# A long-convolution and FFN kernel: K tables by 128 x 80 matmuls, transforms in 64-row tiles, one chain for 640 channels, and a fixed order of steps

## Chip, cores and metric

The kernel runs on one core of one Trainium2 chip. The metric is the device time of one execution in microseconds (us). Executions of one kernel differ by 1 to 2%. A few runs are marked slow (over 1.5% above the fastest of their kernel); comparisons here are of fast runs with fast runs.

Engine names as in the profile: PE is the TensorE matmul, PEld its weight load (which overlaps PE), DVE is VectorE, ACT is ScalarE, POOL is GpSimd, SP is the engine that issues the DMAs (SPq: its queue of issues). "L678" is line 678 of the kernel that the line is taken from, so the same work has different line numbers in different kernels.

## The reference, cut to what matters

```python
# u: [1, 2048, 640];  L = 2048, D = 640 channels, N = 128 states, F = 1728
g = sigmoid((x * gate_w).sum(-1))                       # x = u
K = einsum("dn,dnl,dn->dl", C, exp(dt * A * l), dt * B).real   # a kernel of 2048 taps for each channel
y = irfft(rfft(u padded) * rfft(K padded))[:L] + u * Dskip     # long convolution
b = (gelu(x @ w_gate) * (x @ w_up)) @ w_down            # GeGLU FFN
out = g * y + (1 - g) * b
```

The kernel makes K from two tables by a contraction over the 128 states, with one small product for each group of channels. It then does the convolution by a transform in two stages (A and B), multiplies the spectra of u and K ("mix"), and transforms back (the end of the mix, then "finish"). FFN work fills PE in between.

## The kernel before: the parts that matter

The program is a list of steps. Each has a cost, what it reads and writes, and a rank. A list scheduler inside the kernel's build replays the steps with these costs and writes them out in the order that results; the ranks are the dictionary `P`.

```python
def contract(h):                              # h: half of the channels, W = 320
    ...
                for i in range(16):
                    for q in range(2):
                        for cg in range(4):
                            c = 16 * (b0 + b) + i
                            nc.tensor.matmul(ps[32 * cg:32 * cg + NE, k + b, 32 * i:32 * i + 32],
                                             lhsT=cs2[:, q, c, cg:4 * NE:4],      # 128 x 20 stationary
                                             rhs=cs1[:, q, c, cg:128:4],          # 32 moving columns
                                             start=(q == 0), stop=(q == 1))
    ...                                       # 640 matmuls for a half, 1280 in all
    for e0, n, r0, rs in ((0, 8, 1, 8), (8, 4, 257, 4), ...):        # 5 groups
        for cg in range(4):                   # 20 writes, in runs of 80 channels = 160 bytes
            ... nc.sync.dma_start(out=dst, in_=src)     # dS (in HBM) <- K table

def gathers(h, R): ...                        # 15 reads of dS: spread K over the partitions (Kl)
def stageA(h, R): ...                         # first stage of K's transform, write dKA[h]

def stageB(src, key, dst, name, c, R):        # second stage: 128 x 128 weights
    ...
                for b in range(2):
                    nc.tensor.matmul(ps[:, k + b, 0:W], lhsT=TB[:, 0, :], rhs=bi[s][:, 2 * a + b, :], start=True, stop=True)

u_spec(0, P["U0"])                            # spectrum of u, half 0
stageA(1, P["A1"])
chain(0, P["C0"]); finish(0, P["F0"])         # mix and back transform, half 0
u_spec(1, P["U1"])
chain(1, P["C1"]); finish(1, P["F1"])         # then half 1
plan.run()                                    # the list scheduler fixes the order
plan.emit()
```

Of the kernel before, what the change touches and what calls it, by code (L numbers as in the profile page):

```python
# [12 lines left out]
I32 = mybir.dt.int32  # L13
# [8 lines left out]
X2 = [1, 2, 3, 4, 5, 6, 7, 8, 258, 260, 262, 264, 516, 520, 772, 776, 1032, 1288, 1544, 1800]  # L22
NE = len(X2)


class Plan:
# [50 lines left out]
    def run(self):  # L77
        S = self.steps
        left = [len(s["deps"]) for s in S]
        succ = [[] for _ in S]  # L80
        for s in S:
            for d in s["deps"]:
                succ[d].append(s["i"])
        free, done, aset, line = {}, {}, None, 0
        cand = {}
        ready = {}
        pairs = [0.0] * 4
        owner = {}
        last = None
        warm, cols, wend = False, 0, 3413  # L90

        def arrive(i):
            s = S[i]
            for e in s["engs"]:
                t = 0
                for d in s["deps"]:
                    same = S[d]["eng"] == e and not S[d]["x"]
                    t = max(t, done[d] + (0 if same else S[d]["lat"]))
                ready[i, e] = t
                cand.setdefault(e, set()).add(i)  # L100

        for s in S:
            if not s["deps"]:
                arrive(s["i"])
        order = []
        INF = 1e18
        while len(order) < len(S):
            best = None
            for e, c in cand.items():
                if not c:  # L110
                    continue
                pmin = min(pairs) if e == "PE" else 0
                m = min((max(ready[i, e], pmin) if S[i]["psum"] else ready[i, e]) for i in c)
                t = max(m, free.get(e, 0))
                if best is None or t < best[0]:
                    best = (t, e, pmin)
            t, e, pmin = best
            assert t < INF, "deadlock"
            pick = None
            for i in cand[e]:  # L120
                s = S[i]
                rd = max(ready[i, e], pmin) if s["psum"] else ready[i, e]
                if rd > t:
                    continue
                sc = s["rank"] - s["age"] * (t - ready[i, e]) / 1000
                if s["aset"] not in (None, aset) and e == "ACT":
                    sc += self.switch
                if pick is None or (sc, i) < pick:
                    pick = (sc, i)
            s = S[pick[1]]  # L130
            i = s["i"]
            for e2 in s["engs"]:
                cand[e2].discard(i)
            s["eng"] = e
            s["t"] = t
            ns = s["engs"][e]
            if e == "ACT" and s["aset"] not in (None, aset):
                ns += 1280
                aset = s["aset"]
            if e == "DVE" and last in s["deps"]:  # L140
                ns += 60
            if e == "DVE":
                last = i
            if s["psum"]:
                p = min(range(4), key=lambda q: (pairs[q], q))
                s["k"] = 2 * p
                pairs[p] = INF
                owner[i] = p
            if e == "PE":
                while t >= wend:  # L150
                    warm = cols >= 3072
                    cols = 0
                    wend += 3413
                    if t >= wend + 3413:
                        warm, wend = False, t - t % 3413 + 3413
                rest, ns = ns, 0
                while rest > 0:
                    rate = 1 if warm else 0.5
                    room = wend - t - ns
                    step = min(rest, room * rate)  # L160
                    cols += s["cr"] * step
                    rest -= step
                    ns += step / rate
                    if rest > 0:
                        warm, cols, wend = cols >= 3072, 0, wend + 3413
            free[e] = done[i] = t + ns
            if s["x"]:
                line = max(line, t + ns) + s["x"]
                done[i] = line
            if s["frees"] is not None:  # L170
                f = S[s["frees"]]
                if all(d in done for d in f["rel"]):
                    pairs[owner[f["i"]]] = max(done[d] for d in f["rel"]) + 150
            order.append(s)
            for d in succ[i]:
                left[d] -= 1
                if not left[d]:
                    arrive(d)
        self.order = sorted(order, key=lambda s: (s["t"], s["i"]))
        self.done = done  # L180
        return max(done.values())

    def emit(self):
        for s in self.order:
            s["fn"](s)
# [3 lines left out]
def kernel(  # L189
# [26 lines left out]
    out3 = out.rearrange("b (m p) d -> (b m) p d", p=NPH)  # L216
# [5 lines left out]
    ARENA = 212224  # L222
    arena = mp.tile([128, ARENA // 2], BF16, name="arena")
    ps = pp.tile([128, 8, 512], FP32, name="ps")
    P = dict(sw=5.4, gate=1.91, up=2.5, gelu=8.59, age=0.75, mul=-0.94, un=1.65, uw=1.85, K0=2.33, K1=5.9,
             W=6.08, RT=6.44, ua=0.33, ue=6.48, down=2.99, z=2.89, T2=2.96, A0=6.55, U0=-3.8, A1=2.03, C0=-4.3,
             F0=0.78, U1=1.3, C1=1.89, F1=0.8)
    plan = Plan(P["sw"])
    add = plan.add
# [30 lines left out]
    def mm(n):  # L260
        return n / 2.4 + 4
# [10 lines left out]
    def dma(kb, fn, r=(), w=(), rank=5.0, **k):  # L272
        return add({"SP": 450}, lambda s: fn(), r, w, rank=rank, lat=1900, x=max(100, kb * 3.2), **k)
# [31 lines left out]
    O_TB = O_W + 5120  # L305
    O_WA = O_TB + 768
    O_CS1 = O_WA + 8192
    O_CS2 = O_CS1 + 40960
    O_TRIG = O_CS2 + 25600
    O_PH = O_TRIG + 10240  # L310
    O_A = O_PH + 20480
    O_TAIL = O_A + 8960
# [6 lines left out]
    Wg = [at(O_W + 1280 * k, [128, NKT, 128], BF16, f"Wg{k}") for k in range(2)]  # L319
    Wu = [at(O_W + 2560 + 1280 * k, [128, NKT, 128], BF16, f"Wu{k}") for k in range(2)]  # L320
    TB = at(O_TB, [128, 3, 128], BF16, "TB")
# [16 lines left out]
    vrdt = at(O_TAIL, [N, D], BF16, "vrdt")  # L338
    drow = at(O_TAIL + 1280, [128, D], BF16, "drow")[0:1]
    krow = [drow[:, W * h:W * h + W] for h in range(2)]  # L340
    kst = at(O_TAIL + 2560, [128, 32, 80], BF16, "kst")
    un = at(O_TAIL + 7680, [128, D], BF16, "un")
    ua = [at(O_TAIL + 8960 + 2560 * k, [128, 2, D], BF16, f"ua{k}") for k in range(2)]
    O_TT = O_ZA
    tph = at(O_TT, [128, 2, 512], I32, "tph")
    tsn = at(O_TT + 4096, [128, 2, 512], BF16, "tsn")
    iot = at(O_TT + 6144, [128, 640], I32, "iot")
    tpb = at(O_TT + 8704, [128, 3, 128], I32, "tpb")
# [5 lines left out]
    i4 = cp.tile([128, 4], I32, name="i4")  # L354
    mA = cp.tile([128, 4], FP32, name="mA")
    mQ = cp.tile([128, 4], FP32, name="mQ")
# [8 lines left out]
    dU = [dp.tile([32, 128, W], BF16, name=f"dU{h}") for h in range(2)]  # L365
    dS = [dp.tile([NS, W], BF16, name=f"dS{h}") for h in range(2)]
    dKA = [dp.tile([32, 128, W], BF16, name=f"dKA{h}") for h in range(2)]
    dY = [dp.tile([32, 128, W], BF16, name=f"dY{h}") for h in range(2)]


    kI = iot[:, 0:32]
    tI = iot[:, 32:48]
    k2I = iot[:, 48:112]
    pI = iot[:, 112:240]
    rI = iot[:, 240:368]

    def iotas():
        g = nc.gpsimd
        g.iota(row_i[:], pattern=[[0, 1]], base=0, channel_multiplier=1)
        g.iota(i4[:], pattern=[[1, 4]], base=0, channel_multiplier=0)  # L380
        g.iota(kI, pattern=[[32, 32]], base=8, channel_multiplier=0)
        g.iota(tI, pattern=[[1, 16]], base=0, channel_multiplier=16)
        g.iota(k2I, pattern=[[1, 64]], base=0, channel_multiplier=0)
        g.iota(pI, pattern=[[1, 16], [0, 2], [16, 4]], base=0, channel_multiplier=0)
        g.iota(rI, pattern=[[0, 16], [16384, 2], [0, 4]], base=0, channel_multiplier=0)
        g.memset(ones[:], 1.0)

    pool(2500, iotas, w=["iot", "ones", "ci"])
    jI = tpb.rearrange("p a b -> p (a b)")

    FIELDS = ((0, 3), (5, 31), (0, 31), (3, 31), (2, 1), (0, 63), (6, 1))

    def fields():
        v = nc.vector
        v.memset(b_eps[:], 1e-37)
        for c, (sh, mask) in enumerate(FIELDS):
            v.tensor_scalar(out=fi[:, c:c + 1], in0=row_i[:], scalar1=sh, scalar2=mask, op0=ALU.logical_shift_right,
# [33 lines left out]
    for pl in range(4):  # L431
        ve(v2(1024), lambda pl=pl: expandA(pl), r=["tsn", "fld"], w=[("WA", pl)], rank=RT)
# [278 lines left out]
    def kgen(h):  # L711
        for g in range(4):
            exps1(h, 4 * g, 4)
# [262 lines left out]
```

## Time and profile before

| | before |
|---|---|
| time, median of 3 runs (range) | 345.71 us (344.22 to 348.69) |
| span of the profiled run, granted clock | 344.3 us, 0.92 |
| PE / DVE / ACT busy | 273.3 / 238.2 / 220.5 us |
| DMA queue | 60.23 MB, 61.1% of 16 engines' span |
| instructions on PE: matmuls, weight loads | 2785, 2798 |

These lines are from the page of the kernel before. In part 1, each engine has its busy time, share of the span and count. The row `PE` in part 2 gives busy tenths in 40 slices of 8.6 us; the row `DMA` does the same for the DMA engines. A queue line gives packets, MB and share. The group lines give busy us, the mean ns of one instruction, and the idle time before them with what ended most of it.

```profile
span 344.3 us, 6849 instructions
...
PE 273.3 (79%) x2785; PEld 155.4 (45%) x2798; DVE 238.2 (69%) x331; ACT 220.5 (64%) x302; POOL 4.0 (1%) x15
...
PE   0289999988994699999995267439699999899953
...
DMA  7972222455543223453256529757999799996495
...
q8 instruction: 22, 0.36, 0.4%
...
L678 PE MATMUL ps<-arena 128*20 128x32 bf16 x1280 | 12.7, 198 | 18.6 <-issue 18.6
...
L851 PE MATMUL ps<-arena 128*128 128x320 bf16 x128 | 22.6, 310 | 5.6 <-DMA arena<-dU 3.0
...
L880 PE MATMUL ps<-arena 128*128 128x320 bf16 x128 | 18.7, 299 | 0.0
```

No engine is full. PE is the nearest, with 71 us idle, and its row of tenths dips at four places: the start, slices 13 and 14, slices 23 to 28, and the end. The contraction L678 has only 12.7 us of matmuls but 18.6 us of idle time before them. The profile puts that idle time down to "issue", which means no wait that it can see.

These are stretches of PE's timeline of the kernel before, at the two contractions: start us, length us, group, count, and in brackets the idle time before it.

```profile
110.05 1.25 PE L678 MATMUL ps<-arena 128*20 128x32 bf16 x128 [2.27 <-issue]
...
186.74 1.24 PE L678 MATMUL ps<-arena 128*20 128x32 bf16 x128 [2.14 <-issue]
193.21 1.24 PE L678 MATMUL ps<-arena 128*20 128x32 bf16 x128 [5.23 <-issue]
196.94 1.25 PE L678 MATMUL ps<-arena 128*20 128x32 bf16 x128 [2.48 <-issue]
200.94 0.98 PE L678 MATMUL ps<-arena 128*20 128x32 bf16 x95 [2.75 <-issue]
```

A piece of 128 matmuls takes 1.25 us, and before the next one PE mostly stands for 2 to 3 us, once for 5.2 us. The two contractions occupy about 101.4 to 117.7 and 183.1 to 201.9 us.

The timeline of SP's queue in the kernel before, after the second contraction, shows the issues of the K table's writes (L707) and of the gathers (L821):

```profile
202.82 0.75 SPq L707 DMA_DIRECT2D dS<-arena  x2
...
221.20 5.36 SPq L707 DMA_DIRECT2D dS<-arena  x6
...
229.20 6.05 SPq L821 DMA_DIRECT2D arena<-dS  x7
```

20 small writes (the 21st, a single row, is issued elsewhere), with other DMAs between them, go out from 202.8 to 226.6 us, and the gathers follow until 240.6 us. Until then not all of the second half's K is there to be transformed.

The table of windows of the kernel before gives, for each stretch: its length, busy us (and count) of each engine, the granted clock of PE, the DMA share, and GB/s.

```profile
183.00:201.90 18.90, 6.30 (x642) 5.72 (x642) 2.61 (x3) 3.44 (x5) 0.60 (x1) 0.61 0.45 95
201.90:248.00 46.10, 30.78 (x148) 15.14 (x148) 23.06 (x27) 23.32 (x30) 0.00 (x0) 0.83 0.76 187
...
322.00:344.30 22.30, 13.26 (x85) 8.07 (x83) 10.52 (x20) 0.00 (x0) 0.00 (x0) 0.84 0.75 224
```

PE loses 12.6 us in the second contraction and 15.3 us in the stretch after it, and 9 us at the end. The granted clock is low where PE starves: 0.61 in the stretch of the second contraction. The Trainium skill, "TensorE: Matmul & The Clock Gate", Part 1, says that a PE left idle falls back to half clock, and this agrees: from 190 to 200 us, where PE is busy for only 2.49 us, the granted clock is 0.50.

### The profile page before, as it was taken

How to read it: one execution, taken by the hardware profiler on the slowest of the kernel's cores; microseconds unless marked ns; L12 is line 12 of the kernel's file. 1: busy time of each engine (PE TensorE's matmuls, PEld its weight loads, DVE VectorE, ACT ScalarE, POOL GpSimd, SP SyncE). 2: the span in 40 equal slices, each digit the busy share in tenths (PEclk: the TensorE clock that was granted, in tenths of full speed). 3: DMA queues.
4: the chain of work that ended last, by engine and by line, in shares of the span. 5: the costliest groups of instructions: out<-in, count | busy, mean ns of one | idle time of the engine just before them, and what ended most of it. 6: DMA issues, size and time to landing. Idle time of an engine off the chain costs nothing.

```text
span 344.3 us, 6849 instructions
## 1 busy us (share of the span) xinstructions
PE 273.3 (79%) x2785; PEld 155.4 (45%) x2798; DVE 238.2 (69%) x331; ACT 220.5 (64%) x302; POOL 4.0 (1%) x15
## 2 busy tenths in 40 slices
PE   0289999988994699999995267439699999899953
PEld 0044444433673367544443243214346666566731
DVE  5969887999894258698973044524649865799364
ACT  4999986996894499788995046534547853525200
POOL 3000000000000000000000000000000000000000
PEclk9999999999998589999998569858989999999995
DMA  7972222455543223453256529757999799996495
GB/s 242 343 247 57 77 78 76 134 171 151 155 116 101 66 34 76 131 182 83 76 146 136 105 38 216 167 166 176 307 344 351 243 295 305 256 345 204 165 321 163
DMA packets 57989, 60.66 MB, mean 176 GB/s; under 512 B 9475, under 2 KB 53318, under 8 KB 57926
## 3 DMA queue, kind: packets, MB, share of 16 engines
q1 hardware_dynamic: 57958, 60.23, 61.1%
q8 instruction: 22, 0.36, 0.4%
q14 instruction: 9, 0.07, 0.1%
HBM read 35.80 MB, written 19.17 MB: 160 GB/s over the span
## 4 chain that ended last, share of the span: by engine, by line
PE 49%; DMA 25%; SPq 9%; issue 8%; DVE 4%; ACT 2%; DVEq 0%; ACTq 0%
PE ps L530 16%; PE ps L578 12%; PE ps L550 10%; DMA arena<-dY 8%; PE ps L880 4%; SPq L707 3%; PE ps L678 3%; DMA arena<-dKA 3%; ACT arena L289 2%; DMA arena<-in_params_dram 2%; DMA arena<-in_w_gu_dram 2%; DMA arena<-dU 2%; PE ps L748 2%; DMA arena<-in_u_nat_dram 2%; DMA dKA<-arena 2%
## 5 line engine op out<-in xcount | busy, mean ns | idle before, releaser
L289 ACT CAST arena<-ps 128x640 bf16<-128x640 f32 (+2 forms) x110 | 69.4, 692 | 65.8 <-DVE arena L293 26.1
L530 PE MATMUL ps<-arena 128*128 128x512 bf16 x274 | 65.0, 388 | 16.9 <-DMA arena<-in_w_gu_dram 16.0
L550 PE MATMUL ps<-arena 128*128 128x512 bf16 x253 | 63.1, 397 | 13.8 <-DMA arena<-in_w_gu_dram 10.3
L293 DVE CAST arena<-ps 128x640 bf16<-128x640 f32 (+2 forms) x62 | 48.4, 800 | 36.6 <-PE ps L678 21.7
L578 PE MATMUL ps<-arena 128*128 128x320 bf16 x448 | 65.2, 306 | 0.5 <-ACT arena L289 0.3
L578 PEld LDWEIGHTS <-arena 128*128 128x128 bf16 x448 | 44.6, 100 | 19.6 <-issue 1.3
L530 PEld LDWEIGHTS <-arena 128*128 128x128 bf16 x280 | 27.6, 99 | 50.6 <-DMA arena<-in_w_gu_dram 16.0
L550 PEld LDWEIGHTS <-arena 128*128 128x128 bf16 x260 | 26.2, 101 | 46.9 <-DMA arena<-in_w_gu_dram 11.7
L554 DVE TENSOR_TENSOR arena<-ps,arena 128x1024 bf16<-128x1024 f32 x26 | 31.7, 1219 | 18.6 <-PE ps L550 16.2
L618 ACT ACTIVATE arena<-arena 128x2560 bf16<-128x2560 int16 x18 | 41.6, 2340 | 1.6 <-DVE arena L614 1.5
L534 ACT ACTIVATE arena<-ps 128x1024 bf16<-128x1024 f32 (+1 forms) x28 | 27.1, 1024 | 7.6 <-PE ps L530 7.4
L678 PE MATMUL ps<-arena 128*20 128x32 bf16 x1280 | 12.7, 198 | 18.6 <-issue 18.6
L851 PE MATMUL ps<-arena 128*128 128x320 bf16 x128 | 22.6, 310 | 5.6 <-DMA arena<-dU 3.0
L639 DVE TENSOR_TENSOR arena<-arena 128x2560 bf16<-128x2560 bf16 x16 | 23.0, 1484 | 3.8 <-ACT arena L618 3.8
L628 ACT ACTIVATE arena<-arena 128x320 bf16<-128x320 f32 x64 | 23.2, 454 | 0.9 <-DVE arena L481 0.9
L678 PEld LDWEIGHTS <-arena 128*20 128x20 bf16 x1280 | 11.3, 99 | 20.3 <-issue 20.3
L295 DVE TENSOR_SCALAR arena<-ps,omg 128x640 bf16<-128x640 f32 x9 | 7.9, 882 | 18.0 <-PE ps L578 17.9
L851 PEld LDWEIGHTS <-arena 128*128 128x128 bf16 x128 | 12.5, 101 | 14.7 <-DMA arena<-dU 3.8
L880 PE MATMUL ps<-arena 128*128 128x320 bf16 x128 | 18.7, 299 | 0.0
L904 DVE SCALAR_TENSOR_TENSOR arena<-ps,g_f,arena 128x320 bf16<-128x320 f32 x32 | 15.4, 544 | 2.7 <-PE ps L898 2.7
L666 DVE TENSOR_TENSOR arena<-arena 128x2560 bf16<-128x2560 bf16 x10 | 14.9, 1486 | 3.2 <-ACT arena L618 3.1
L612 DVE SCALAR_TENSOR_TENSOR arena<-arena 128x320 int32<-128x320 f32 x40 | 16.9, 483 | 0.0
(89 smaller groups left out, 225.2 us busy)
## 6 DMA issues: line engine op xcount, KB each, us to landing
arena<-in_w_gu_dram SPq DMA_DIRECT2D x52, 160.0 KB
dU<-arena SPq DMA_DIRECT2D x32, 160.0 KB
arena<-dU SPq DMA_DIRECT2D x8, 640.0 KB
arena<-arena SPq DMA_DIRECT2D x16, 320.0 KB
dKA<-arena SPq DMA_DIRECT2D x8, 640.0 KB
arena<-dKA SPq DMA_DIRECT2D x8, 640.0 KB
dY<-arena SPq DMA_DIRECT2D x8, 640.0 KB
arena<-dY SPq DMA_DIRECT2D x8, 640.0 KB
```

The costliest lines, as they stand in the source:

```text
L289: nc.scalar.copy(out=dst, in_=src(b))
L293: nc.vector.tensor_copy(out=dst, in_=src(b))
L530: nc.tensor.matmul(ps[:, k + j, :], lhsT=Wg[w][:, kt, :], rhs=xT[2 * grp + j][:, kt, :], start=(kt == 0), stop=(kt == NKT - 1))
L534: add({"ACT": an(1024)}, lambda s: nc.scalar.activation(out=HTall[0:p, :, f, :], in_=ps[0:p, plan.bank(g):plan.bank(g) + 2, :], func=ACT.G ...
L550: nc.tensor.matmul(ps[:, k + j, :], lhsT=Wu[w][:, kt, :], rhs=xT[2 * grp + j][:, kt, :], start=(kt == 0), stop=(kt == NKT - 1))
L554: add({"DVE": v1(1024)}, lambda s: nc.vector.tensor_tensor(out=HTall[:, :, f, :], in0=ps[:, plan.bank(u):plan.bank(u) + 2, :], in1=HTall[: ...
L578: nc.tensor.matmul(ps[:, k + h, 0:W], lhsT=HTq[q][:, f, 128 * j:128 * j + 128], rhs=Wd[f][:, W * h:W * h + W], start=(f == 0), stop=(f == ...
L618: ac(an(2 * n * W), lambda: nc.scalar.activation(out=t[:], in_=ph.bitcast(I16)[:, :, :, 0:32:2], func=ACT.Sin, scale=SIN_SCALE), r=[f"ph{k ...
L628: nc.scalar.activation(out=cs1[:, 1, :, 4 * s:4 * s + 4], in_=quads(aT[:, ds]), func=ACT.Exp, scale=float(sg * (4 + 8 * i)))
L678: nc.tensor.matmul(ps[32 * cg:32 * cg + NE, k + b, 32 * i:32 * i + 32], lhsT=cs2[:, q, c, cg:4 * NE:4], rhs=cs1[:, q, c, cg:128:4], start= ...
L851: nc.tensor.matmul(ps[:, k + b, 0:W], lhsT=TB[:, 0, :], rhs=bi[s][:, 2 * a + b, :], start=True, stop=True)
L880: nc.tensor.matmul(ps[:, k + b, 0:W], lhsT=TB[:, m, :], rhs=x[:, 2 * a + b, :], start=(m == 1), stop=(m == 2))
```

## The change

The intent is to turn the 1280 tiny matmuls into 320 larger ones, to write the K table in 640-byte runs, to do the 64-point transforms in 64-row tiles of the array (four at once), to merge the two chains of 320 channels into one of 640 with longer runs, and to replace the list scheduler by a fixed table of 920 steps. The diff, cut to its core:

```diff
+ORDER = [int(v) for v in """
+    336 1392 652 276 12 296 356 436 ...          # 920 numbers: step * 20 + engine * 4 + PSUM pair
+""".split()]
 class Plan:
-    def run(self):                               # the list scheduler goes
-        ...
     def emit(self):
-        for s in self.order:
+        for v in ORDER:
+            s = self.steps[v // 20]
+            assert s["deps"] <= seen
             ...
 def contract(h):
-    for i in range(16): for q in range(2): for cg in range(4):
-        matmul(ps[32*cg:32*cg+NE, ...32 columns], lhsT=cs2[:, q, c, cg:4*NE:4], rhs=cs1[:, q, c, cg:128:4])
+    for i in range(n): for x in range(2):
+        matmul(ps[:, ...80 columns], lhsT=cs1[:, x, k0 + i, :], rhs=cs2[:, x, k0 + i, :])
+    ... 16 "pick" matmuls with a selection matrix put the wanted fourth of the rows into kst2
-    20 writes to dS, runs of 160 bytes
+    4 writes to dS, runs of 640 bytes                       # and one row each, as before
 def stageB(...):
-    for b in range(2):
-        matmul(ps[:, k + b, 0:W], lhsT=TB[:, 0, :], rhs=bi[s][:, 2 * a + b, :])
+    for y in range(2): for x in range(2):                     # four 64 x 64 tiles
+        matmul(ps[64*y:64*y+64, k + x, 0:W], lhsT=TB[64*x:64*x+64, 0, :], rhs=t[64*x:64*x+64, 2*a + y, HV[h]])
-chain(0); finish(0); u_spec(1); chain(1); finish(1)
+for c in range(8): mix(...)                                  # all 640 channels, 1280-byte runs
+finish(ys, ...)                                              # reads dY only after all of it is written
```

Gathers go from 15 to 18 issues a half, the weights of the FFN get three buffers instead of two, and dU is written in 2560-byte runs. Nothing else of the arithmetic changes.

## The prediction

> **What bounds the kernel now.** No engine is full: the page gives PE 273 us of 344 (79%), DVE 238, ACT 220, DMA queues 61%. The table of windows shows where PE's 71 idle us lie. (a) 0-25 us: first gate matmuls at about 13-16 us, then a stop until 25 us for a w_gu tile. (b) The two contractions of the K tables (L678): 1280 matmuls are only 12.7 us busy but 101.5-117 and 183-201 us on the clock, since they stop five or so times for about 2.5 us of "issue" (18.6 us), and the granted clock falls to 0.50 there (110-120, 190-200). (c) After the second one the chain of waits is a file of SP issues (21 small dS writes, then 15 gathers, 205-241 us) with PE at 0.5 of 10 us in 220-230. (d) From 240 to 310 us the DMA share is 1.0 at 246-345 GB/s; (e) the end, 322-344, is write dY, read dY, finish, store.
>
> **What changes.**
> - Contraction: 1280 matmuls of 20 columns by 32 become 320 of 128 by 80 and 32 picks. Estimate 10 us each instead of 16 and 18,: about -14 us, all on the chain. Price: evictions of 8000 instead of 2560 columns per half, at the traced 0.7-0.8 us per 640 about +13 us over ACT and DVE.
> - dS writes 21 to 5 issues per half with 640 B runs instead of 160 B (the 9475 packets under 512 B go); gathers 15 to 18 issues. Contraction to filled K shrinks from about 39 to about 25 us, and the fixed table puts u-spectrum, gate/up and K0 work over it.
> - 64-row tiles: the back transforms and mixes (L851, L880, L898: 22.6 + 18.7 + 11.1 us busy) do half the array work. The Trainium skill, "TensorEngine Tiling (Array Packing)", Key Properties, says that tiles run independently and that a mode switch drains the array. The trace agrees with the first (1280 column tiles at 9.9 ns each); nothing here prices the drain. Estimate -15 to -20 us of PE, mostly hidden behind DMA.
> - DMA: bytes stay near 60 MB; dU is written in 2560 B and read in 1280 B runs (before 640 and 5120). At 305 GB/s little moves.
> - Merging the chain gives something back: all of dY (5.2 MB) must be written before it is read. After the last mix come 7.8 MB plus latencies, estimate 33 us, where the second half alone took 22.
> - Start: three gates and the logits come first; the 20-25 us stop should go, but ACT and DVE set the first contraction, so little comes through.
>
> **Sum.** Adding traced durations in the table's order, ACT and DVE need about 95 us to the first contraction (near 103 us, as now) and about 165 us to the second (near 183, as now, but with some 13 us more gate/up work done by then). From there about 29 MB, 97 us at 300 GB/s, against about 91 us of PE, then about 5 us of stalls and the 33 us end: 318. A few us for drains and cold clock: 321 us, 8 times in 10 between 307 and 337. Faster by over 2%: 0.84; within: 0.11; slower: 0.05.
>
> **What would show it.** Each contraction about 10 us; no long PE gap between the second contraction and its K transform; tiled groups of four 320-column matmuls in 0.13-0.2 us; DMA near 1.0 from about 225 us; an end of 30-35 us without PE.
>
> **What would make it wrong.** Tiles that don't overlap, or costly drains (+20 us); evictions delaying the tables; a DMA backlog from swaps and merged dY; or a fixed order overtaken by real delays.

## The result

| | before | after |
|---|---|---|
| median (range), same rounds | 347.2 us (344.22 to 349.3) | 327.56 us (326.74 to 330.13) |
| ratio of fast runs | | 0.9453, 95% interval 0.9357 to 0.9549 |
| span of the profiled run, granted clock | 344.3 us, 0.92 | 325.8 us, 0.92 |

A ratio here and below is the mean time of one kernel's fast runs over that of the kernel before in the same rounds, so it is not quite the ratio of the medians. The change is 5.5% faster. The time lies in the predicted range, 6.6 us above its centre.

The page after, with the same kinds of lines:

```profile
span 325.8 us, 5490 instructions
...
PE 266.1 (82%) x2112; PEld 146.7 (45%) x2126; DVE 246.3 (76%) x332; ACT 223.6 (69%) x307; POOL 5.3 (2%) x18
...
PE   0799999897796999979899987985998889993452
...
DMA  6993344332321144433437659979366569934997
...
q8 instruction: 16, 0.26, 0.3%
...
L807 PE MATMUL ps<-arena 64*64 64x320 bf16 x256 | 16.9, 325 | 9.0 <-DMA arena<-dKA 2.8
...
L854 PE MATMUL ps<-arena 128*64 128x320 bf16 x64 | 10.2, 474 | 14.5 <-DMA arena<-dY 14.5
...
L650 PE MATMUL ps<-arena 128*128 128x80 bf16 x320 | 13.5, 212 | 3.8 <-DVE arena L637 2.8
```

PE's busy time falls by only 7 us, although the tiled groups (L807, L834 and L854, 39.6 us in all) cost 12.8 us less than L851, L880 and L898 did (52.4). DVE and ACT rise by 11.2 us together, mostly for the larger evictions (copies from PSUM): those of the contraction and the picks went from about 7 to about 19 us. The dip of PE's row at the second contraction is gone; at the first, one slice of 6 tenths is left. The dip at the end is longer: finish (L854) waits 14.5 us for dY. The idle time before the contraction is 3.8 us, and none of it stands at "issue".

PE's timeline after, at the two contractions and at two tiled groups:

```profile
100.36 7.48 PE L650 MATMUL ps<-arena 128*128 128x80 bf16 x160 [2.79 <-DVE arena L637]
...
182.32 4.46 PE L650 MATMUL ps<-arena 128*128 128x80 bf16 x120 [0.49 <-ACT arena L504]
...
187.83 1.59 PE L650 MATMUL ps<-arena 128*128 128x80 bf16 x40 [0.51 <-DVE arena L247]
...
260.63 0.60 PE L807 MATMUL ps<-arena 64*64 64x320 bf16 x12
261.58 0.33 PE L807 MATMUL ps<-arena 64*64 64x320 bf16 x4 [0.35 <-ACT arena L245]
```

The contractions take 7.5 and 7.1 us with nothing standing still inside a piece, and they begin at 100.4 and 182.3 us, almost where they began before (101.4 and 183.1).

SP's queue after, first behind the second contraction (L678 here is a dS write, L744 and L752 are gathers), then at the end (dY writes L840, dY reads L847):

```profile
199.09 2.10 SPq L678 DMA_DIRECT2D dS<-arena  x4
...
206.07 9.16 SPq L744 DMA_DIRECT2D arena<-dS  x10
...
289.93 7.48 SPq L840 DMA_DIRECT2D dY<-arena  x3
300.74 5.57 SPq L847 DMA_DIRECT2D arena<-dY  x5
```

The table's writes are out in 2.1 us, and the last gather is issued by 220.3 instead of 240.6 us. At the end the first read of dY cannot be issued before the last write has landed.

The table of windows after:

```profile
190.10:238.50 48.40, 39.03 (x275) 18.11 (x278) 25.43 (x30) 25.84 (x40) 1.05 (x1) 0.93 0.77 232
238.50:294.60 56.10, 50.06 (x582) 32.58 (x583) 42.43 (x42) 31.89 (x49) 1.04 (x1) 0.97 0.73 243
294.60:325.80 31.20, 11.54 (x96) 5.07 (x88) 15.38 (x19) 1.29 (x2) 0.00 (x0) 0.57 0.77 279
```

The stretch behind the contraction now has PE at 39.0 of 48.4 us, where it was 30.8 of 46.1. The last 31.2 us have PE at 11.5, where the last 22.3 had 13.3.

The 18.5 us between the two profiled spans can be split by these stretches. The second contraction begins 0.7 us earlier (182.3 instead of 183.0), it takes 11.1 us less (7.8 instead of 18.9), and what follows takes 6.7 us less (135.7 instead of 142.4). The first contraction also takes 9.5 us less (7.6 instead of 17.1), but that does not bring the second one forward. So far this looks like the predicted story. The experiments agree with only part of it.

### The profile page after: what moved, and what is told of

It reads as the page before. It is cut to its first block, busy times and chain, and to the rows that moved or that the text cites. A ratio compares the mean times of both kernels' runs of the same rounds, so it can differ in the third digit from the quotient of the medians.

```text
span 325.8 us, 5490 instructions
## 1 busy us (share of the span) xinstructions
PE 266.1 (82%) x2112; PEld 146.7 (45%) x2126; DVE 246.3 (76%) x332; ACT 223.6 (69%) x307; POOL 5.3 (2%) x18
## 4 chain that ended last, share of the span: by engine, by line
PE 36%; ACT 22%; DVE 18%; DMA 15%; issue 5%; SPq 3%; DVEq 0%; ACTq 0%
PE ps L548 13%; PE ps L520 8%; PE ps L500 7%; ACT arena L243 6%; ACT arena L589 5%; DVE arena L247 5%; DMA dKA<-arena 4%; ACT arena L599 4%; DMA arena<-dY 3%; DMA arena<-dU 3%; ACT arena L504 3%; DMA arena<-dKA 2%; DVE arena L859 2%; PE ps L650 2%; PE ps L807 2%
## 5 line engine op out<-in xcount | busy, mean ns | idle before, releaser
L243 ACT CAST arena<-ps 128x640 bf16<-128x640 f32 x111 | 70.6, 702 | 38.1 <-PE ps L807 15.7
L500 PE MATMUL ps<-arena 128*128 128x512 bf16 x276 | 66.5, 392 | 13.0 <-DMA arena<-in_u_T_dram 9.2
L247 DVE CAST arena<-ps 128x640 bf16<-128x640 f32 (+2 forms) x67 | 56.2, 881 | 20.1 <-PE ps L807 10.4
L520 PE MATMUL ps<-arena 128*128 128x512 bf16 x250 | 63.1, 401 | 4.2 <-DVE arena L524 1.9
L548 PE MATMUL ps<-arena 128*128 128x320 bf16 x448 | 65.0, 305 | 1.0 <-DVE arena L247 0.5
L548 PEld LDWEIGHTS <-arena 128*128 128x128 bf16 x448 | 44.5, 100 | 20.6 <-issue 2.1
L520 PEld LDWEIGHTS <-arena 128*128 128x128 bf16 x260 | 26.5, 103 | 37.2 <-issue 9.3
L807 PE MATMUL ps<-arena 64*64 64x320 bf16 x256 | 16.9, 325 | 9.0 <-DMA arena<-dKA 2.8
L599 ACT ACTIVATE arena<-arena 128x320 bf16<-128x320 f32 x64 | 23.3, 455 | 1.0 <-DVE arena L451 1.0
L854 PE MATMUL ps<-arena 128*64 128x320 bf16 x64 | 10.2, 474 | 14.5 <-DMA arena<-dY 14.5
L859 DVE SCALAR_TENSOR_TENSOR arena<-ps,g_f,arena 128x640 bf16<-128x640 f32 x16 | 13.0, 878 | 11.9 <-PE ps L854 11.9
L627 ACT ACTIVATE arena<-arena 128x320 bf16<-128x320 f32 x40 | 14.8, 455 | 5.9 <-PE ps L650 5.9
L582 DVE SCALAR_TENSOR_TENSOR arena<-arena 128x320 int32<-128x320 f32 x40 | 16.9, 483 | 0.8 <-ACT arena L589 0.7
L650 PE MATMUL ps<-arena 128*128 128x80 bf16 x320 | 13.5, 212 | 3.8 <-DVE arena L637 2.8
L807 PEld LDWEIGHTS <-arena 64*64 64x64 bf16 x256 | 8.2, 107 | 17.7 <-issue 9.7
L650 PEld LDWEIGHTS <-arena 128*128 128x128 bf16 x320 | 13.3, 107 | 4.6 <-DVE arena L637 3.5
L780 PE MATMUL ps<-arena 128*128 128x320 bf16 x64 | 12.1, 308 | 4.1 <-DMA arena<-dS 2.3
```

Of the source, the lines that this page charges most:

```text
L243: nc.scalar.copy(out=dst, in_=src(b))
L247: nc.vector.tensor_copy(out=dst, in_=src(b))
L500: nc.tensor.matmul(ps[:, k + j, :], lhsT=Wg[w][:, kt, :], rhs=xT[2 * grp + j][:, kt, :], start=(kt == 0), stop=(kt == NKT - 1))
L520: nc.tensor.matmul(ps[:, k + j, :], lhsT=Wu[w][:, kt, :], rhs=xT[2 * grp + j][:, kt, :], start=(kt == 0), stop=(kt == NKT - 1))
L548: nc.tensor.matmul(ps[:, k + h, 0:W], lhsT=HTq[q][:, f, 128 * j:128 * j + 128], rhs=Wd[f][:, W * h:W * h + W], start=(f == 0), stop=(f == ...
L599: nc.scalar.activation(out=cs1[:, 1, :, 4 * s:4 * s + 4], in_=quads(aT[:, ds]), func=ACT.Exp, scale=float(sg * (4 + 8 * i)))
```

## The experiments

All twelve kernels gave the reference's result, also those that do extra work on purpose. They ran in three calls, the first two on one chip and the third (s1b, s4, e5, e8) on another; the kernel before had medians of 344.52, 346.08 and 345.03 us in the rounds of the first, second and third call. A median in the table is of all four runs; s3 has two slow runs among them and e5 one.

| run | what it is | median us | ratio to before [95%] |
|---|---|---|---|
| (after) | the whole change | 327.56 | 0.9453 [0.9357, 0.9549] |
| e1 | after, every tiled matmul twice | 334.33 | 0.9716 [0.9637, 0.9795] |
| e2 | before + new contraction, list order | 352.42 | 1.0224 [1.0152, 1.0296] |
| e3 | after, list order | 343.68 | 0.9977 [0.9926, 1.0029] |
| e6 | after, 640-byte runs in the chain | 329.77 | 0.9565 [0.9489, 0.9640] |
| s1 | before, searched table | 348.32 | 1.0077 [1.0010, 1.0145] |
| s2 | e2, searched table | 323.22 | 0.9345 [0.9293, 0.9396] |
| s3 | after, another searched table | 335.40 | 0.9607 [0.9526, 0.9688] |
| e4 | after, half of dY read early | 331.53 | 0.9604 [0.9528, 0.9680] |
| s1b | before, searched longer | 351.60 | 1.0207 [1.0139, 1.0274] |
| s4 | after, but two chains; searched table | 325.53 | 0.9439 [0.9365, 0.9513] |
| e5 | after, 160-byte dS writes | 337.16 | 0.9771 [0.9685, 0.9857] |
| e8 | after, old contraction added | 356.37 | 1.0356 [1.0287, 1.0425] |

The theory at the outset was the prediction's: the contraction and the dS file make the gain, and the tiles and the order add little. The rivals were that the tiles make it, and that the order makes it.

### e2: the contraction part alone

This is the kernel before with the new contraction, picks, dS writes and gathers, and nothing else of the change. The list scheduler and its ranks stay.

```diff
 # kernel before
-def contract(h): 640 matmuls 128*20, 20 dS writes
+def contract(h): 160 matmuls 128*128, 16 picks, 4 dS writes     # as in the kernel after
-def gathers: 15 issues
+def gathers: 18 issues                                          # as in the kernel after
```

> The kernel before with only the new contraction (320 matmuls of 128 by 80, the picks), the four 640-byte dS writes and the new gathers; everything else, its scheduler and its two chains stay. My theory (contraction and the file of SP issues behind it are most of the gain): 12 to 18 us faster than before, about 330. Rival (tiles, run lengths or the order table are the gain): less than 6 us faster. It should give the right result.

It is 2.2% slower than the kernel before (all of the interval lies above 1, but it spans 2%). The theory that this part alone brings 12 to 18 us fell. The contraction itself does what it should: its trace shows 160 matmuls in 5.90 us from 192.49 us on. The time is lost behind it. This is PE's timeline of this run, the down projection of the FFN:

```profile
217.75 26.65 PE L584 MATMUL ps<-arena 128*128 128x320 bf16 x195
```

and this is its table of windows around that:

```profile
222.00:242.00 20.00, 20.00 (x149) 14.41 (x148) 4.99 (x6) 0.00 (x0) 0.00 (x0) 1.00 0.20 44
...
282.00:322.00 40.00, 25.65 (x145) 15.01 (x145) 31.87 (x42) 15.60 (x26) 0.00 (x0) 0.87 1.01 299
```

The order runs 195 matmuls of the down projection in one block. K's transform waits behind it, although the last gather was issued by 226.4 us, and the first write of dKA goes out at 246.1, as SP's queue shows:

```profile
246.11 2.78 SPq L865 DMA_DIRECT2D dKA<-arena  x3
```

Meanwhile the DMA engines stand at a share of 0.20. Afterwards they are full at 1.01 for 40 us, and PE has only 25.65 busy us there. The faster contraction did not shorten the whole, because the order that the ranks of the kernel before give puts this block ahead of K's transform.

### e3: the whole change in the list scheduler's order

```diff
 # kernel after
-ORDER = [...]                     # the fixed table
+def run(self): ...                # the list scheduler of the kernel before, with the kernel's own costs and ranks
```

> The changed kernel with the fixed table taken out and the list scheduler of before put back, on the changed kernel's own ranks. If the table only records what that scheduler gives: within 2 us of 327.6 and the same order. If the table itself is a large part of the gain: 8 us or more slower. I expect 2 to 8 us slower.

The whole change without its table is as fast as the kernel before. The table is worth 16 us by the medians. PE's timeline of this run shows the largest single loss:

```profile
218.31 0.48 PE L857 MATMUL ps<-arena 64*64 64x320 bf16 x4 [11.55 <-DVE arena L297]
```

SP's queue at that time, and DVE's timeline:

```profile
206.62 12.14 SPq L870 DMA_DIRECT2D arena<-arena  x3
...
221.75 0.33 SPq L728 DMA_DIRECT2D dS<-arena  x1
...
217.27 2.45 DVE L297 CAST arena<-ps 128x800 bf16<-128x800 f32 x3 [11.55 <-DMA arena<-arena]
```

Three swaps of the u spectrum (L870) stand ahead of the dS writes (L728), and they occupy the queue for 12.1 us. But the queue is not what held the writes back. The K table's picks ended at 206.4 us on PE, and their evictions (the casts of 128x800) waited for the landing of swaps: DVE's began at 217.27, when one had landed at 217.15, and ACT's at 220.89, when the last had landed at 220.79. The first write went out at 221.75, released by ACT's eviction. PE and the third swap in the queue waited behind DVE's. So this order puts swaps where the table's last steps must wait for them; which buffer ties the two I did not isolate.

### s1, s1b, s2: is it the table alone, or the contraction with a table?

e2 and e3 leave two readings: the table is the whole gain, or the table and the structure need one another. So I searched orders for the kernel before and for e2 with the same effort. The kernel's own list scheduler was replayed with step costs set to durations from the traces, the ranks of single steps were varied at random and kept when the replayed end came earlier (about a million orders each), and the best order was written as a fixed table. The replay only chooses; it is not a time. For s1 it said 328, and the chip said 348; for s1b 323, and the chip said 352.

```diff
-    plan.run()                    # s1, s1b: kernel before;  s2: e2
+ORDER = [...]                     # a searched table, written out as in the kernel after
```

> The kernel before with nothing changed but its order: its list scheduler is replaced by a fixed table, found by a search over the ranks of single steps, with the step costs set to the durations of these traces. The removal of the changed kernel's table cost 16 us, so the order may be the gain. Theory O (order alone): 326 to 332 us. Theory S (the structure is needed, the order only lets it show): 336 to 345. The replayed costs of the search say 328, an estimate that was within 4 us for three of the four kernels run so far and 5 off for the fourth.

> The kernel before with the new contraction, dS writes and gathers (which with the old ranks was 2% slower than before), now with a table searched in the same way and for as long as the one above. Theory S: the difference to the table of the kernel before is what the contraction is worth: 10 to 18 us less than that run, about 315 to 320. Theory O: no more than 4 us less than that run.

> A second table for the kernel before, searched twice as long, with the old contraction and its dS writes costed as the trace of the first table showed them (15.5 and 16.3 us, about 1 us per issue). The replayed costs say 323. Theory S (no order takes the stalls of the 1280 matmuls and the file of 21 writes off the chain): 338 us or more. Theory O (the first table was only a bad one): 332 us or less.

The kernel before gains nothing from a searched table (348.32 us). s1b searched longer, with the costs of the contraction and of the dS writes set to what they take on the chip, and is no better (351.60 us). The same search on e2 takes 29 us off e2 and gives 323.22 us, the fastest kernel: 6.5% faster than before. It has no tiles, no merged chain and no third weight buffer.

s1's timeline of PE shows that a table does not remove the stops of the old contraction:

```profile
184.74 1.24 PE L628 MATMUL ps<-arena 128*20 128x32 bf16 x128 [2.48 <-issue]
```

s2's has none:

```profile
178.30 5.90 PE L639 MATMUL ps<-arena 128*128 128x80 bf16 x160
```

and SP's queue of s2 has the dKA writes early: these four go out from 217.60 us on, where e2's began at 246.1:

```profile
217.60 7.66 SPq L815 DMA_DIRECT2D dKA<-arena  x4
```

So in these runs neither part is worth anything alone: contraction alone +7.9 us by the medians (e2), table alone +2.2 (s1) or +6.6 (s1b). Together they are worth 22.9 us (s2).

One limit remains. A search can only show that it found no better order for the kernel before, not that there is none. And it chose by a replay that was 20 and 29 us too low for the kernel before, against 12 to 14 us for s3 and s4 (fast runs), so it had the worse guide there.

### e8: what the old contraction costs in a fixed order

```diff
 # kernel after, in contract(h), same order table
+    for i in range(n):            # the old matmuls first, into the same PSUM; overwritten by the new ones
+        for x in range(2): for cg in range(4):
+            matmul(ps[32*cg:32*cg+NE, ...], lhsT=cs2[:, x, k0 + i, cg:4*NE:4], rhs=cs1[:, x, k0 + i, cg:128:4])
     for i in range(n):
         for x in range(2): matmul(...)          # new
```

> The changed kernel with the old contraction's 1280 matmuls of 20 columns by 32 put in front of its own (their result is overwritten, so it stays right), same order. If the old contraction is 15 us of chain each time: 24 to 36 us slower, 352 to 364, with stops of about 2 us after every 128 matmuls. If it could run beside other work: less than 12 us slower.

It costs 28.8 us by the medians (9.0% of the time before, or 31 us, by the ratios), about 14.4 for each contraction, inside what was expected. In the trace the two contractions, old and new together, last 21.0 and 21.6 us, where the new one alone took 7.5 and 7.1. PE's timeline of this run (L651 are the old matmuls, L656 the new ones):

```profile
107.92 0.20 PE L651 MATMUL ps<-arena 128*20 128x32 bf16 x2 [1.30 <-issue]
108.05 1.03 PE L656 MATMUL ps<-arena 128*128 128x80 bf16 x24
109.02 0.97 PE L651 MATMUL ps<-arena 128*20 128x32 bf16 x96
109.92 0.39 PE L656 MATMUL ps<-arena 128*128 128x80 bf16 x6
111.65 0.82 PE L656 MATMUL ps<-arena 128*128 128x80 bf16 x18 [1.34 <-issue]
```

The stop at 111.65 us comes after 2 + 24 + 96 + 6 = 128 matmuls, of whatever shape, so after 256 instructions, since each matmul has its weight load. That is a count of instructions, not of work, and it points at the line `q8 instruction` of the page. The Trainium skill, "Advanced Engine Details and Errata", ISA Cache, says that an engine's instructions are held in lines of 16 KB, which are 256 instructions. This agrees: the packets of that queue have 16,384 bytes each in the trace. The kernel before loads 22 of them, and 22 x 256 = 5632 against its 5583 PE instructions; after it is 16, or 4096, against 4238; e8 has 26, or 6656, against 6798. The stops of e8 are 0.65 to 2.14 us, mostly shorter than the 2 expected; new matmuls lie between the old ones here.

The trace also has each packet's time. In the kernel before, these are the packets around the contractions and the moments at which PE goes on after a stop, both from the start of the span in us:

```
packet starts   103.74  107.48  111.34  114.83 |  184.10  190.51  194.36  198.44
PE goes on      106.32  110.05  113.77  117.50 |  186.74  193.21  196.94  200.94
difference        2.58    2.57    2.43    2.67 |    2.64    2.70    2.58    2.50
```

PE goes on 2.4 to 2.7 us after a packet has started, also after the one stop of 5.2 us. In e8 the same holds for all eleven stops in and just behind the two contractions, with 2.2 to 2.9 us. So PE's stops are waits for its own next 256 instructions, as far as a coincidence in time, nineteen times over, can show it. While PE uses them up faster, a block arrives every 3.5 to 4 us (once 6.4), which is about 14 ns for an instruction (3.5 us / 256). The old contraction used 256 in 1.25 us, 5 ns each. The new one uses 320 in 7.48 us, 23 ns each, and never stops. e2 and s2 use 320 in 5.90 us, 18 ns each, and don't stop either.

### e5: narrow dS writes

```diff
 # kernel after, same order table
-dma(... S[1+160*g:161+160*g, :] <- kst2[32*g:32*g+32])                     # 4 writes a half, 640-byte runs
+for j in range(4): dma(... S[..., 80*j:80*j+80] <- kst2[32*g:32*g+32, :, j, :])   # 16 writes, 160-byte runs
```

> The changed kernel with its dS writes cut back to 160-byte runs: 16 issues per half instead of 4, same bytes, same order. 12 more issues at 0.6 to 1 us in front of the gathers of the second half. If the file of issues lies on the chain there: 4 to 9 us slower, 332 to 337. If the work laid over it hides it: within 2 us of 327.6.

Its three fast runs have a median of 335.86 us, 8.3 us slower and inside what was expected (with the slow run the median is 337.16; the ratios give 11 us). SP's queue of this run:

```profile
202.78 9.46 SPq L678 DMA_DIRECT2D dS<-arena  x16
```

The 16 writes hold the queue for 9.46 us, where 4 took 2.10. The first gather of that group moves from 206.07 to 217.80 us. The file of issues is a real term, as predicted. An issue holds the queue for nearly the same time in both runs (0.59 and 0.53 us), so the queue fills with the count of issues. What the shorter runs cost at landing is not separated from this.

### e1: twice the tiled work

```diff
 # kernel after: stageB, the mix and finish
+for again in range(2):
     for y in range(2): for x in range(2): matmul(...)      # in the mix: (U, Us, U, Us) instead of (U, Us)
```

> The changed kernel with every matmul of the 64-row and 64-column tiles done twice (the second pass overwrites the first, so the result stays right); the array streams as many columns in these steps as the kernel before did. From the runs x4, x8, x12 of the trace after (0.33, 0.47, 0.60 us) a group of four costs 0.135 us more, so this adds about 160 groups x 0.135 = 21 us of PE. My theory (the tiles' saving is mostly hidden behind DMA and evictions): time up by 3 to 9 us over 327.6. Rival (the halved array work is the gain): up by 16 us or more, back to about 345.

The time rises by 6.8 us (by the ratios 2.6%, or 9 us). That was expected. The page of this run has

```profile
L808 PE MATMUL ps<-arena 64*64 64x320 bf16 x512 | 24.1, 301 | 4.5 <-DVE arena L247 1.6
```

where L807 had 16.9 us. The three tiled groups together go from 39.6 to 57.4 us, so 17.8 us of PE were added, near the 21 expected. (PE's whole busy time rises by only 11.8, from 266.1 to 277.9, since other lines took less in this run, L520 59.1 us instead of 63.1; its granted clock was 0.95 instead of 0.92.) Of the 17.8 us, 6.8 to 9 came out in the time, so half or somewhat more was hidden. If the saving of 12.8 us comes through in the same share, an estimate that no run tests, the tiles are worth 5 to 6.5 us in this order: not nothing, and not the main part.

The two L807 lines of the timeline after show how the tiles run. Four matmuls of 64 x 64 and 320 columns take 0.33 us between other work, 8 take 0.47 and 12 take 0.60 us in one stretch, so each further four cost about 0.135 us, which is about the time of one matmul (a stretch of 28 untiled ones of 320 columns takes 3.96 us in the same trace, 0.141 us each). The Trainium skill, "TensorEngine Tiling (Array Packing)", Key Properties, says that tiles run in parallel and that a mode switch needs a drain. Both show here. The first is the 0.135 us for four. The 0.33 us of a lone group do not show the second, since a lone untiled matmul of 320 columns is listed with 0.30 us. The starts of the matmuls do: in the trace after, one of 320 columns starts 136 ns after the one before it in the same mode, and 229 ns after it where the mode changes to tiles without a wait. So a switch costs about 93 ns, and the kernel after has 35 changes of mode on PE: about 3 us in all, an estimate from these numbers.

### e6: short runs in the merged chain

```diff
 # kernel after: loads of dU and dKA, writes of dY
-dma(t <- v[:, CS*c:CS*c+CS, :])                    # 1280-byte runs
+for hv in HV: dma(t[:, :, hv] <- v[:, CS*c:CS*c+CS, hv])    # two DMAs of 640-byte runs
```

> The changed kernel with its 1280-byte runs cut to 640 (loads of dU and dKA and writes of dY issued once per half of the channels): 15.7 MB in twice as many packets and 24 more issues. My theory (run lengths move little at about 300 GB/s): 2 to 6 us slower. Rival (the 1280-byte runs are a main source of the gain): 12 us or more slower. Right result.

It is 2.2 us slower by the medians, at the lower edge of what was expected: the longer runs are a small part. (By the ratios it is 1.1%, or 4 us.)

### e4: the end of the merged chain

In the kernel after, "finish" reads all of dY after all of it is written. This kernel reads the 64 rows of the first four chunks early and only the other 64 at the end.

```diff
 # kernel after, with the early reads moved up in the order table
-dma(t <- dY[:, 4*g:4*g+4, :])                                       # waits for all 8 chunks
+for z in range(2): dma(t[64*z:64*z+64] <- dY[64*z:64*z+64, 4*g:4*g+4, :])   # z = 0 waits for chunks 0-3
```

> The changed kernel with the reads of dY split into the rows of chunks 0 to 3 and of chunks 4 to 7; the first half is issued after the fourth and sixth later writes, into eight buffers instead of four, so that after the last mix 2.6 MB are read instead of 5.2. If the end of the merged chain is bound by DMA: 2.6 MB at 0.33 to 0.36 MB per us, 6 to 8 us less, about 320 to 322. If it is bound by the finish on PE and DVE (13 us busy there) or by the stores: 0 to 3 us less.

It is 4 us slower, where 6 to 8 us faster was expected. SP's queue of this run, the last write of dY (L839) and the reads that wait for it (L847):

```profile
298.29 0.37 SPq L839 DMA_DIRECT2D dY<-arena  x1
306.71 3.00 SPq L847 DMA_DIRECT2D arena<-dY  x5
```

From the issue of the last write to the first read that needs it are 8.4 us. In the kernel after, the last write was issued at 297.05 us, and its landing, at 300.25, released the read at 300.74. Four early reads were issued at 294.03 to 297.9, just ahead of the write. The Trainium skill, "DMA: Bandwidth & Descriptors", Queues, rings and completion order, says that each DMA engine consumes its descriptors in ring order; the 8.4 us against 3.7 agree with that. While the later reads and the stores ran (310 to 322 us), the DMA engines moved 206 to 285 GB/s, where they moved 312 to 421 in the kernel after (302 to 322 us). A read taken in advance of the write that everybody waits for was no gain here.

### s3 and s4: other tables, and two chains

s3 is the kernel after with a table from my search. s4 keeps the tiles and the new contraction but has the two chains by halves, as the kernel before, also with a searched table.

```diff
 # s3: kernel after
-ORDER = [... as in the change ...]
+ORDER = [... searched ...]
 # s4: kernel after, CS = 8 chunks of 320 channels, dKA and dY by halves
-mix(all 8 chunks of 640); finish(all)
+mix(half 0); finish(half 0); mix(half 1); finish(half 1)      # with a searched table
```

> The whole change with a table of my search in place of its own. If my search is as good as the one that made the table: at most 328. The replayed costs say 318 (its own table: 332, measured 327.6), so I expect 314 to 324. If it is over 332 my search can't be compared with the table, and the two runs above say less.

> The changed kernel with its 64-row tiles and its contraction, but with the chain by halves of the channels as before (chunks of 8 by 320, dKA and dY per half), and a table searched in the same way. The replayed costs say 314; merged they said 318 (measured 335) and with the change's own table 332 (measured 327.6). If merging costs at the end and the tiles save PE: 312 to 320, under the 323 of the run that has the contraction alone. If tiles bring nothing: 322 to 330.

s3 took 335.40 us, but two of its four runs, the profiled one among them, were slow. Its two fast runs took 331.65 and 332.88 us. The same structure moves by about 5 us with the table (the ratios, too, give 5), and my search was worse than the change's author's here. s4 took 325.53 us, inside the 322 to 330 that was expected if the tiles bring nothing.

s2, s4 and the kernel after share the contraction and have a good table each, and they lie within 4.4 us of one another, 323.2 to 327.6. That is no more than a table alone made between s3 and the kernel after. So these runs give no gain to the tiles and the merged chain. They do not show that there is none: which of the three structures is best with the best order for each stays open.

## Why the prediction was right, and where it was not

The time was right, and the direction with it. The account of it was only partly right.

**Right.**
- The two starts: ACT and DVE set the first contraction. I said 103 us and about 183 us for the second; the trace has 100.4 and 182.3.
- The contraction's cost, in kind; the size was too small: I put the whole part at -14 us, all on the chain. It fell from 17.1 and 18.9 us (the windows from 100.6 and from 183.0) to 7.6 and 7.8, so by 20.6 in these two stretches. I said 10 us each; the trace has 7.5 and 7.1. Only the second one's 11.1 us show in the span, since the second contraction began no earlier. e8 shows that in this order the old matmuls' time comes out in full, 28.8 us for both.
- The dS file: a real wait, 8.3 us in e5.
- The tiles: I said 15 to 20 us of PE, mostly hidden. It was 12.8 us of busy time, and e1 shows half or somewhat more of such time hidden. What I left unpriced, the drain, is about 3 us.
- The end: I said 33 us. The trace has 31.2, from 294.6 to 325.8.
- The evictions: I said +13 us over ACT and DVE; they took about 12 us more (DVE and ACT as a whole 11.2).

**Wrong.** The step that failed is the order's. I wrote that "the fixed table puts u-spectrum, gate/up and K0 work over it", as a help to the structure's gain, and gave it no cost of its own, as if the structure kept its gain in any order. e2 shows the contraction with 7.9 us lost in a list order with the ranks of another kernel. e3 shows the whole change with nothing gained in the list order. The searched tables (s1, s1b) show nothing gained for the old structure. As far as these orders go, the gain belongs to the pair. My sum came out right because I added the durations "in the table's order", so the table was in the sum without a term of its own.

The sum in its terms, after the second contraction begins:

| term | predicted | measured |
|---|---|---|
| second contraction begins | 183 | 182.3 |
| from there to the last mix | 97 + 5 | 112.3 (182.3 to 294.6) |
| end | 33 | 31.2 |
| drains and cold clock | 3 | (in the above) |
| sum | 321 | 325.8 (profiled span) |

The term that was too small is the middle one, by about 7 us with the allowance counted to it. I had it bound by DMA, 29 MB at 300 GB/s with a share near 1.0 from 225 us on. The windows show 232 and 243 GB/s and shares of 0.77 and 0.73, so about 25 MB over the two long stretches (232 x 48.4 + 243 x 56.1). PE was busy for 39.0 + 50.1 of their 104.5 us. With 1.2 MB in the contraction's own stretch that is 26 MB, which at 300 GB/s would be 87 us. So I had too many bytes and too high a rate. The two errors partly cancel, and that the term is only 7 us off is in part luck. What bounded it was neither full DMA nor full PE, but waits between them; which of these waits cost the 7 us I did not isolate.

Also missed: from the contraction to a filled K I said about 25 us. The last gather is issued at 220 us, 38 us after the contraction began and 30 after it ended. Before, the last one was issued 38.7 us after it ended. Tiled groups of four: I said 0.13 to 0.2 us. It is 0.135 within a stretch, and a change of mode adds 0.09.

And of the stops of the old contraction I knew only "issue". The instruction packets of the trace point to their cause, and I did not look there.

## What to carry to other kernels

A structure and the order of its steps are one thing to tune: a faster part in the old order can cost time, and it should be judged only with an order searched for it, as should the version without it. Count the instructions of a burst of tiny matmuls: here 256 of them came every 3.5 to 4 us, so more than one in 14 ns or so made PE wait, however small they were. Put the write that everything waits for ahead of reads that are merely early, since they share the queue.

## What the Trainium skill lacked or had wrong

- "Advanced Engine Details and Errata", ISA Cache, has the lines of 256 instructions, but no rate at which they come. "Runtime: NRT & Kernel Launch", Instruction fetch mechanics, has none either, and does not count a burst of small instructions among the cases in which the fetch is not hidden. Here a line of PE instructions came every 3.5 to 4 us; 256 of them used in 1.25 us made PE stand for 2 to 3 us each time, once for 5.2, and the profile called it "issue".
- "TensorEngine Tiling (Array Packing)", Key Properties, says that a mode switch drains the array, with no size. Here a matmul of 320 columns started 136 ns after the one before it, and 229 ns after it where the mode changed to 64 x 64 tiles: about 93 ns a switch.
- "DMA: Bandwidth & Descriptors" has rates by size, but I found no cost measured on this chip for the time in which many small writes hold the issuing queue. Here 16 writes with 160-byte runs held it for 9.46 us, and 4 with 640-byte runs for 2.10 us, so 0.5 to 0.6 us each.
